# The last twelve chunks of a gated-attention kernel pass the FFN in groups of four, and the second product swaps its operands

## The chip, the cores and the metric

The kernel runs on one NeuronCore of one Trainium2 chip. The metric is the device time of one execution in microseconds; less is better. TensorE (PE) does the matrix products, VectorE (DVE), ScalarE (ACT) and GpSimd (POOL) the elementwise work, and SyncE (SP) issues every DMA of this kernel.

## The reference

Gated linear attention with a state of 48x48 for each head, and then a two-layer feed-forward network (FFN) on all 3072 tokens. Everything is float32.

```python
# q, k, v, alpha: 4 batches, 8 heads, 768 steps, 48 dims
for t in range(S):
    state = alpha[:, :, t, :, None] * state + einsum('bhd,bhe->bhde', k[:, :, t], v[:, :, t])
    y[:, :, t] = einsum('bhd,bhde->bhe', q[:, :, t], state)
x = y.transpose(0, 2, 1, 3).reshape(3072, 384)
h = x @ w_in                       # 384 -> 2048
g = h              where h >= 1
    0              where h <= -1
    (h + 1)**2 / 4 elsewhere
return g @ w_out                   # 2048 -> 384
```

## The kernel before

The 3072 tokens are cut into 24 chunks of 128. `prepare(j)` loads a chunk's alpha, k, q and v and forms running products of alpha with two scans on DVE (L547, L573). `attend(j)` computes the attention of the chunk on PE (transposes L614, scores L629, state updates L642, outputs L769) and `end_chunk` writes it into `ring`, as a high and a low part of each number in the type float32r (L793 on ACT, L798 on DVE). `ring` holds two groups of chunks.

The FFN takes the chunks in groups of `GROUP` = 3, eight groups in all. For each group `n` and each of the 16 slices `f` of 128 hidden units:

- `hidden(n, f)` makes the slice of `h` for the whole group in one PSUM bank, with nine matmuls (L865): three slices of the contraction, and for each the products high x high, low x high and high x low. The stationary operand is a 128x128 piece of `w_in`, the moving one is the group's 384 columns of `ring`. A split, f = 0 of group 0 (`SPLIT` = 1), takes the chunks one at a time, with 128 columns. Then five elementwise operations follow: L909 (DVE), L894 (ACT), L920 (DVE), L924 (ACT, the high part `gh[:, 0]`) and L925 (POOL, the low part `gh[:, 1]`; on DVE for the very last slice).
- `second(seg, f)` adds the slice's part of the output to three PSUM banks `ps_o`, one for each chunk, again with nine matmuls (L943). Here `gh` of one chunk (128x128) is stationary, and the 384 columns of `w_out` move. After the last slice each bank is copied to `ot` (L340, on ACT or DVE) and written to `out` by a DMA (L1002).

Groups 0 and 1 pass the first eight slices before the weights of the other eight are decoded; their partial sums wait in DRAM (`sums`). The weights are fetched and decoded in the first part of the kernel on ACT, DVE and POOL (L365 to L420).

The order of the instructions on each engine is written out by a planner (`Plan.order`). Each operation has a key (for the FFN a running count of slices, for a chunk's attention a due time some `MARGIN` slices before its group begins) and an estimated cost. The planner simulates the engines with these costs and, whenever an engine is free, takes the ready operation with the smallest key. Where PE would rest in the early part, it inserts matmuls on zeros (`fill`, L1014). PSUM's eight banks go to `ps_h` (2), `ps_o` (`GROUP`) and the attention (`6 - GROUP`). If an overflow test fails, a slow version (`stepwise`) is run; it isn't with these inputs.

Of the kernel before, what the change touches and what calls it, by code (L numbers as in the profile page):

```python
# [8 lines left out]
F32 = mybir.dt.float32  # L9
F32R = mybir.dt.float32r  # L10
# [15 lines left out]
SLACK = 2.0**-15  # L26
GROUP = 3
SHARE = 2
# [14 lines left out]
FIRST = 5  # L43
ROOM = 2
# [188 lines left out]
def gated_attention_ffn(ctx: ExitStack, tc: tile.TileContext, q, k, v, alpha, laid, out):  # L233
    nc = tc.nc
    B, H, S, D = q.shape
    P = 128
    DM, DF = H * D, laid["w_out"].shape[0] * laid["w_out"].shape[2] // (H * D) * P
    G = H // 2
    KT = DM // P
    NF = DF // P  # L240
    CH = 128
# [51 lines left out]
    span = lambda n: slice(first[n] % (2 * GROUP), first[n] % (2 * GROUP) + groups[n])  # L293
    meet = const.tile([P, NCH, 2, G], F32, name="meet")
# [5 lines left out]
    segs += [(n, 0, NF) for n in range(NS, NG)]  # L300
    starts = [sum(f1 - f0 for _, f0, f1 in segs[:i]) for i in range(len(segs))]

    begin = {n: starts[[s[0] for s in segs].index(n)] for n in range(NG)}
    need = {}
    for (n, f0, f1), t in zip(segs, starts):
        for f in range(f0, f1):
            need.setdefault(f // NW, t + f - f0)


    wts = ctx.enter_context(tc.tile_pool(name="wts", bufs=2 * NU + MORE))  # L310
    with ExitStack() as main:
# [26 lines left out]

        ps_a = lambda j, *shape: bank("ps_a", 6 - GROUP, [P, *(shape or (G, CH))], FIRST, j < ROOM)
        copy = lambda e, out, in_: (nc.scalar.copy if e == "ACT" else nc.vector.tensor_copy)(out=out, in_=in_)  # L340
# [260 lines left out]
        others, meets, turnt = {}, {}, {}  # L601
        group_of = [max(n for n in range(NG) if first[n] <= j) for j in range(NCH)]

# [182 lines left out]
        def end_chunk(j, ps, key):  # L786

            n = group_of[j]
            xt = ring[:, j % (2 * GROUP)]
            GS = KT if n == 0 else G  # L790
            hi, lo = xt[:, 0:GS, 0], xt[:, 0:GS, 1]
            x_j = ("x", j % (2 * GROUP))
            plan.op("ACT", 0.14 * GS, key, lambda: nc.scalar.copy(out=hi, in_=ps()[:, 0:GS]), [ps], [x_j])  # L793
# [11 lines left out]
            x = ring[:, span(n)].bitcast(F32)  # L805
            all_x = [("x", i % (2 * GROUP)) for i in range(first[n], j + 1)]
            for kt in range(KT):
# [42 lines left out]


        def hidden(n, f, key, c0=0, c1=GROUP):

            c1 = min(c1, groups[n])
            L = (c1 - c0) * CH
            h = bank("ps_h", 2, [P, L])
            gf, gh = buf("fw", "gf", [P, L], 3), buf("fw", "gh", [P, 2, L], 3, F32R)
            xs = [("x", j % (2 * GROUP)) for j in range(first[n] + c0, first[n] + c1)]
# [29 lines left out]

            w = (c1 - c0) / GROUP
            act = lambda in_, func, scale, bias: plan.op(  # L890
# [3 lines left out]
                lambda: nc.scalar.activation(out=gf(), in_=in_(), func=func, scale=scale, bias=bias),  # L894
                [h, gf] if in_ is gf else [h],
                [gf],
            )
            if key < CLIPS:


                act(h, AF.Relu, -0.5, half_b)
                act(gf, AF.Relu, -1.0, ones)
                act(gf, AF.Square, 1.0, 0.0)
            else:
                plan.op(
                    "DVE",
                    0.08 + 0.45 * w,
                    key + 0.4,
                    lambda: nc.vector.tensor_scalar(  # L909
                        out=gf(), in0=h(), scalar1=-1.0, scalar2=1.0, op0=ALU.max, op1=ALU.min  # L910
                    ),
                    [h],
                    [gf],
                )
                act(gf, AF.Square, 0.5, half_b)
# [4 lines left out]
                lambda: nc.vector.tensor_tensor(out=gf(), in0=gf(), in1=h(), op=ALU.max),  # L920
                [gf, h],
                [gf],
            )
            plan.op("ACT", 0.08 + 0.41 * w, key + 0.4, lambda: nc.scalar.copy(out=gh()[:, 0], in_=gf()), [gf], [gh])  # L924
# [4 lines left out]
            plan.op(e, us, key + 0.4, emit, [gf, gh], [gh], port=port, other=None if ends else other)  # L929
            return gh  # L930

        o_ps, seconds, firsts = {}, {}, []

        def second(seg, f, gh, key, c0=0, c1=GROUP):
            n, f0, f1 = seg
            c1 = min(c1, groups[n])
            if f == f0 and c0 == 0:
                o_ps[seg] = [bank("ps_o", GROUP, [P, DM]) for _ in range(groups[n])]

            def product(ts):  # L940
                for t in ts:
                    for i, (a, w) in enumerate(((0, 0), (0, 1), (1, 0))):
                        nc.tensor.matmul(  # L943
                            out=o_ps[seg][t](),
                            lhsT=gh()[:, a, (t - c0) * CH : (t - c0 + 1) * CH],
                            rhs=wout(f, w),
                            start=(f == f0 and i == 0),
                            stop=(f == f1 - 1 and i == 2),
                        )

            ts = range(c0, c1)

            for part in [[t] for t in ts] if f == f1 - 1 else [ts]:
                seconds[seg, f] = plan.op(
                    "PE",
                    0.529 * len(part),
                    key,
                    lambda part=part: product(part),
                    [gh, wo[f // NW]],
                    [o_ps[seg][t] for t in part],  # L960
                    mode="full",
                )
            if f < f1 - 1:
                return
            for t in ts:
                ps, ot = o_ps[seg][t], buf("fw", "ot", [P, DM], GROUP)
                place = ("sums", n, t)
                if f0 > 0:
# [3 lines left out]
                        key - 6,  # L972
                        lambda t=t, ot=ot: nc.sync.dma_start(out=ot(), in_=sums[n, t]),
                        [place],
                        [ot],
                        moved=P * DM * 4,
                        after=[seconds[seg, f - 3]],
                    )
                    plan.op(
                        "DVE",  # L980
                        0.52,
                        key,
                        lambda ps=ps, ot=ot: nc.vector.tensor_tensor(out=ot(), in0=ot(), in1=ps(), op=ALU.add),
                        [ps, ot],
                        [ot],
                    )
                else:
                    plan.op(
                        "ACT",
                        0.45,  # L990
                        key,
                        lambda ps=ps, ot=ot: copy("ACT", ot(), ps()),
                        [ps],
                        [ot],
                        other=("DVE", 0.52, lambda ps=ps, ot=ot: copy("DVE", ot(), ps()), False),
                    )
                r0 = (first[n] + t) * CH
                plan.op(
                    "SP",
                    Plan.ISSUE,  # L1000
                    key,
                    lambda t=t, r0=r0, ot=ot: nc.sync.dma_start(  # L1002
                        out=out[r0 : r0 + CH, :] if f1 == NF else sums[n, t], in_=ot()
                    ),
                    [ot],
                    [place],
                    moved=P * DM * 4,
                )
# [12 lines left out]
        for j in range(NCH):  # L1021
# [6 lines left out]
            while at < len(segs) and first[segs[at][0]] + groups[segs[at][0]] - 1 <= done:  # L1028
                seg, t = segs[at], starts[at]
                at += 1  # L1030
                for f in range(seg[1], seg[2]):
                    key = t + f - seg[1]
                    parts = range(groups[0]) if seg[0] == 0 and f < SPLIT else [0]
# [47 lines left out]
def stepwise(tc, q, k, v, alpha, win, wout, NF, ident, half_b, ones, out):  # L1081
# [8 lines left out]
    with ExitStack() as ctx:  # L1090
# [39 lines left out]
        with tc.For_i(0, B * S, P) as r:  # L1130
# [12 lines left out]
            for kt in range(KT):  # L1143
# [3 lines left out]
                nc.vector.tensor_tensor(out=xt[:, 1, kt], in0=tr, in1=xt[:, 0, kt].bitcast(F32), op=ALU.subtract)  # L1147
            o = ps.tile([P, DM], F32, name="o")
            for f in range(NF):
# [18 lines left out]
                nc.vector.tensor_tensor(out=gh[:, 1], in0=g, in1=gh[:, 0].bitcast(F32), op=ALU.subtract)  # L1168
                for i, (a, w) in enumerate(((0, 0), (0, 1), (1, 0))):
                    nc.tensor.matmul(  # L1170
                        out=o,
                        lhsT=gh[:, a],
                        rhs=wout(f, w),
                        start=(f == 0 and i == 0),
                        stop=(f == NF - 1 and i == 2),
                    )
            ot = sb.tile([P, DM], F32, name="ot2")
            nc.vector.tensor_copy(out=ot, in_=o)
            nc.sync.dma_start(out=out[bass.ds(r, P), :], in_=ot)

# [62 lines left out]
```

## Time and profile before

| | before |
|---|---|
| time, median of 3 runs | 521.03 us (520.73 to 521.82) |
| span of the profiled execution | 520.1 us |
| PE busy | 498.7 us, 96% |
| PE weight loads (PEld) busy | 480.4 us, 92% |
| DVE, ACT, POOL busy | 69%, 51%, 51% |
| granted PE clock | 1.0 of full speed in nearly all of the span |

The page does not give the profiled execution a time of its own beside the span; the median of the three runs is 0.9 us above the span, which is taken for what lies around it. In the views a line such as L943 is line 943 of the kernel before, `x9` counts instructions, and a window A:B is in microseconds from the start of the span. A matmul's own duration runs from its issue to its modelled end and overlaps with the next ones; what one matmul costs in a stream is the distance from start to start.

### The profile page before, as it was taken

Reading aid. Unit: us, or ns where it says so; the run is one execution under the profiler, and the core shown is the slowest. Engines: PE = TensorE matmul, PEld = TensorE weight load, DVE = VectorE, ACT = ScalarE, POOL = GpSimd, SP = SyncE. Lnnn points to the kernel's source line nnn. Section 1 sums busy time; section 2 is a strip of 40 time slices with the busy share of each in tenths; the row PEclk is TensorE's granted clock in tenths of the full one; section 3 lists DMA queues with packets and bytes.
Section 4 is the critical chain, followed back from the end, with each engine's and each line's share of the span. In section 5 each row is a group of like instructions: output and inputs, shape, how many; then the busy total and the mean of one; then the engine's idle time right before and its main releaser. Section 6 shows DMA issues by size and latency. Waiting matters only on the chain.

```text
span 520.1 us, 12248 instructions
## 1 busy us (share of the span) xinstructions
PE 498.7 (96%) x4861; PEld 480.4 (92%) x4861; DVE 359.6 (69%) x673; ACT 262.8 (51%) x509; POOL 262.9 (51%) x286
## 2 busy tenths in 40 slices
PE   8889898979999999999999999999999999999995
PEld 7788788978899999999999999999999999999994
DVE  6999999788978757578567757578567775343333
ACT  3899896575543444344444444444444444333331
POOL 3688885899974354254354344254354242323330
PEclk9999999999999999999999999999999999999999
DMA  8997849011435323133123323133102200010001
GB/s 255 378 348 250 316 98 346 3 48 55 122 106 137 109 65 90 48 96 122 43 60 91 112 62 79 56 84 125 56 21 59 67 2 11 15 37 10 0 1 50
DMA packets 27902, 52.46 MB, mean 101 GB/s; under 512 B 3808, under 2 KB 13504, under 8 KB 27840
## 3 DMA queue, kind: packets, MB, share of 16 engines
q1 hardware_dynamic: 27840, 51.62, 31.8%
q8 instruction: 40, 0.66, 0.6%
q14 instruction: 22, 0.18, 0.1%
HBM read 43.65 MB, written 5.90 MB: 95 GB/s over the span
## 4 chain that ended last, share of the span: by engine, by line
PE 79%; DVE 9%; POOL 4%; issue 3%; ACT 3%; DVEq 0%; POOLq 0%; ACTq 0%
PE ps L943 35%; PE ps L865 34%; PE ps L769 4%; PE ps L642 2%; DVE inv L573 2%; POOL gh L925 2%; PE ps L629 2%; PE ps L614 2%; DVE Q L547 1%; POOL w L405 1%; ACT gf L894 1%; DVE w L381 1%; DVE Q L715 1%; POOL wt L420 1%; PE ps L1014 1%
## 5 line engine op out<-in xcount | busy, mean ns | idle before, releaser
L943 PE MATMUL ps<-wt,gh 128*128 128x384 f32 x1152 | 225.3, 340 | 4.3 <-POOL gh L925 3.5
L925 POOL TENSOR_TENSOR gh<-gf,gh 128x384 fp32r<-128x384 f32 (+1 forms) x129 | 146.6, 1141 | 163.6 <-ACT gh L924 117.2
L865 PE MATMUL ps<-ring,wt 128*128 128x384 f32 (+1 forms) x1170 | 223.0, 337 | 2.8 <-DVE inv L573 1.2
L865 PEld LDWEIGHTS ps<-ring,wt 128*128 128x128 f32 x1170 | 203.9, 188 | 4.3 <-issue 1.5
L943 PEld LDWEIGHTS ps<-wt,gh 128*128 128x128 f32 x1152 | 200.5, 188 | 7.2 <-POOL gh L925 5.2
L894 ACT ACTIVATE gf<-gf,half_b 128x384 f32<-128x384 f32 x122 | 74.6, 616 | 120.7 <-DVE gf L909 117.4
L909 DVE TENSOR_SCALAR gf<-ps 128x384 f32<-128x384 f32 x122 | 66.9, 553 | 71.3 <-PE ps L865 62.7
L920 DVE TENSOR_TENSOR gf<-gf,ps 128x384 f32<-128x384 f32 (+1 forms) x130 | 70.3, 543 | 45.1 <-ACT gf L894 44.7
L924 ACT CAST gh<-gf 128x384 fp32r<-128x384 f32 (+1 forms) x130 | 65.7, 507 | 67.8 <-DVE gf L920 61.1
L573 DVE TENSOR_TENSOR_SCAN inv<-raw,bwd 128x511 f32<-128x511 f32 x17 | 34.9, 2052 | 0.0
L405 POOL TENSOR_TENSOR w<-w,wt 128x384 int32<-128x384 int32 (+1 forms) x25 | 31.2, 1261 | 7.0 <-DVE w L392 6.0
L547 DVE TENSOR_TENSOR_SCAN Q<-raw,fwd 128x512 f32<-128x512 f32 x17 | 27.4, 1613 | 7.3 <-PE ps L769 7.2
L420 POOL TENSOR_TENSOR wt<-w,wt 128x384 fp32r<-128x384 f32 (+1 forms) x24 | 31.3, 1318 | 1.7 <-ACT wt L418 1.4
L661 ACT COPY both<-state 48x192 f32<-48x192 f32 x69 | 24.1, 350 | 12.3 <-POOL state L746 9.0
L746 POOL TENSOR_TENSOR state<-state,last 128x192 f32<-128x192 f32 x20 | 11.9, 594 | 34.3 <-DVE state L671 34.1
L769 PE MATMUL ps<-Q,both 128*64 128x64 f32 x372 | 27.1, 225 | 1.4 <-issue 1.4
L769 PEld LDWEIGHTS ps<-Q,both 128*64 128x64 f32 x372 | 23.7, 137 | 4.1 <-issue 2.8
L769 PE MATMUL ps<-other,both 128*64 128x64 f32 x372 | 27.0, 225 | 0.0
L617 ACT COPY ks<-ps 128x512 f32<-128x512 f32 x24 | 14.1, 587 | 21.5 <-PE ps L614 21.4
L715 DVE TENSOR_TENSOR Q<-ps,mask 64x256 f32<-64x256 f32 x48 | 20.3, 423 | 6.5 <-ACT other L679 5.6
L593 POOL TENSOR_TENSOR Q<-Q,raw 128x512 f32<-128x512 f32 x18 | 23.2, 1290 | 2.9 <-DVE inv L565 2.0
L769 PEld LDWEIGHTS ps<-other,both 128*64 128x64 f32 x372 | 23.5, 138 | 0.2 <-ACT both L661 0.2
(79 smaller groups left out, 415.7 us busy)
## 6 DMA issues: line engine op xcount, KB each, us to landing
both<-in_laid_v_both SPq DMA_DIRECT2D x48, 128.0 KB, 3.0
wt<-in_laid_w_in SPq DMA_DIRECT2D x8, 768.0 KB, 7.2
wt<-in_laid_w_out SPq DMA_DIRECT2D x8, 768.0 KB, 7.5
vt<-in_laid_v SPq DMA_DIRECT2D x24, 192.0 KB, 2.9
out<-ot SPq DMA_DIRECT2D x24, 192.0 KB, 2.7
raw<-in_laid_dim_a SPq DMA_DIRECT2D x17, 256.0 KB, 2.9
raw<-in_laid_dim_k SPq DMA_DIRECT2D x17, 256.0 KB, 3.0
raw<-in_laid_dim_q SPq DMA_DIRECT2D x17, 256.0 KB, 2.7
```

The lines of the kernel that those rows point to most:

```text
L405: add = lambda e, c=c: e.tensor_tensor(out=bits()[:, c], in0=bits()[:, c], in1=word(I32, 0)[:, c], op=ALU.add)
L420: sub = lambda e, c=c: e.tensor_tensor(out=part(1)[:, c], in0=data()[:, c], in1=part(0).bitcast(F32)[:, c], op=ALU.subtract)
L547: lambda: nc.vector.tensor_tensor_scan(flat(Q()), aT(), flat(fwd), 0.0, ALU.mult, ALU.max),
L573: lambda: nc.vector.tensor_tensor_scan(flat(inv())[:, 0:n][:, ::-1], aT()[:, 1 : n + 1][:, ::-1], flat(bwd)[:, 0:n][:, ::-1], bwd[:, G - 1 ...
L769: nc.tensor.matmul(out=ps()[halves[r], to, halves[u]], lhsT=lhsT[:, r, u], rhs=x()[:, g, halves[u]], start=m + u == 0, stop=True, skip_gro ...
L865: nc.tensor.matmul(out=h(), lhsT=win(f, w)[:, kt], rhs=ring[:, at, kt, a, :], start=(m == 0), stop=(m == 3 * KT - 1),)
L894: lambda: nc.scalar.activation(out=gf(), in_=in_(), func=func, scale=scale, bias=bias),
L909: lambda: nc.vector.tensor_scalar(out=gf(), in0=h(), scalar1=-1.0, scalar2=1.0, op0=ALU.max, op1=ALU.min),
L920: lambda: nc.vector.tensor_tensor(out=gf(), in0=gf(), in1=h(), op=ALU.max),
L924: plan.op("ACT", 0.08 + 0.41 * w, key + 0.4, lambda: nc.scalar.copy(out=gh()[:, 0], in_=gf()), [gf], [gh])
L925: sub = lambda e: e.tensor_tensor(out=gh()[:, 1], in0=gf(), in1=gh()[:, 0].bitcast(F32), op=ALU.subtract)
L943: nc.tensor.matmul(out=o_ps[seg][t](), lhsT=gh()[:, a, (t - c0) * CH : (t - c0 + 1) * CH], rhs=wout(f, w), start=(f == f0 and i == 0), sto ...
```

## The change

Groups 0 to 3 stay at three chunks; the last twelve chunks form three groups of four instead of four groups of three. `ring` becomes 2 x 4 chunks long, and its slots go by group. In the second product the operands are swapped: a 128x128 piece of `w_out` is stationary and `gh` of the whole group moves, so that the output comes out transposed (384 x tokens) in three banks `ps_o`, one for each slice of 128 output features; numpy transposes it back on the host. The keys of the planner advance by 4/3 for each slice of a group of four, and the planner's costs are written for both sizes. A smaller scratch area for dynamic DMAs is asked for.

```diff
-GROUP = 3
+SIZES = (3, 3, 3, 3, 4, 4, 4)
+GROUP = max(SIZES)
...
-    groups = [min(GROUP, NCH - j) for j in range(0, NCH, GROUP)]
+    groups = list(SIZES)
...
+    slot = lambda j: group_of[j] % 2 * GROUP + j - first[group_of[j]]
+    span = lambda n: slice(slot(first[n]), slot(first[n]) + groups[n])
...
+    unit = [c / 3 for c in groups]
+    starts = [sum((f1 - f0) * unit[n] for n, f0, f1 in segs[:i]) for i in range(len(segs))]
...
-        sums = pools["sums"].tile([max(NS, 1), GROUP, P, DM], F32, name="sums")
+        sums = pools["sums"].tile([max(NS, 1), KT, P, GROUP * CH], F32, name="sums")
...
-        ps_a = lambda j, *shape: bank("ps_a", 6 - GROUP, ...
+        ps_a = lambda j, *shape: bank("ps_a", 6 - KT, ...
...
+        cost = lambda c: 9 * max(c * 0.0533 + 0.0155, 0.111)
...   (in hidden)
-                    (0.529 if c1 - c0 > 1 else 0.7) * (c1 - c0),
+                    cost(c1 - c0),
...   (in second)
-                o_ps[seg] = [bank("ps_o", GROUP, [P, DM]) for _ in range(groups[n])]
+                o_ps[seg] = [bank("ps_o", KT, [P, groups[n] * CH]) for _ in range(KT)]
-            def product(ts):
-                for t in ts:
+            def product(ms):
+                for m in ms:
                     for i, (a, w) in enumerate(((0, 0), (0, 1), (1, 0))):
                         nc.tensor.matmul(
-                            out=o_ps[seg][t](),
-                            lhsT=gh()[:, a, (t - c0) * CH : (t - c0 + 1) * CH],
-                            rhs=wout(f, w),
-                            start=(f == f0 and i == 0),
+                            out=o_ps[seg][m]()[:, c0 * CH : c1 * CH],
+                            lhsT=wout(f, w)[:, m * P : (m + 1) * P],
+                            rhs=gh()[:, a, 0 : (c1 - c0) * CH],
+                            start=(f == f0 and i == 0 and c0 == 0),
                             stop=(f == f1 - 1 and i == 2),
...
-                    0.529 * len(part),
+                    cost(c1 - c0) / KT * len(part),
...
-                        out=out[r0 : r0 + CH, :] if f1 == NF else sums[n, t], in_=ot()
+                        out=out[m * P : (m + 1) * P, cols] if f1 == NF else sums[n, m, :, 0:L], in_=ot()
...   (on the host)
-    nc = bacc.Bacc("TRN2", target_bir_lowering=False, num_devices=1)
+    nc = bacc.Bacc("TRN2", target_bir_lowering=False, num_devices=1, dynamic_dma_scratch_size=1024)
-    return r.results[0]["out"]
+    return np.ascontiguousarray(r.results[0]["out"].T)
```

## Rows read from the trace of the kernel before

**Rows 1.** The page's parts 1 and 4: busy time by engine, and the chain of work that ended last, by engine and by line.

```profile
PE 498.7 (96%) x4861; PEld 480.4 (92%) x4861; DVE 359.6 (69%) x673; ACT 262.8 (51%) x509; POOL 262.9 (51%) x286
PE 79%; DVE 9%; POOL 4%; issue 3%; ACT 3%; DVEq 0%; POOLq 0%; ACTq 0%
```

**Rows 2.** Busy time of each engine in stretches of the span, with the granted clock, the share of the DMA engines and GB/s.

```profile
30.00:36.00 6.00, 4.66 (x114) 3.86 (x109) 5.79 (x12) 5.85 (x15) 4.55 (x6) 1.00 1.04 358
42.00:48.00 6.00, 5.36 (x108) 4.74 (x104) 5.54 (x8) 5.88 (x12) 5.19 (x7) 1.00 0.62 188
48.00:54.00 6.00, 4.38 (x38) 4.06 (x40) 5.56 (x14) 5.86 (x12) 4.99 (x6) 1.00 0.93 360
...
80.00:120.00 40.00, 35.00 (x279) 33.22 (x278) 33.88 (x57) 26.62 (x48) 33.65 (x27) 1.00 0.36 128
120.00:130.00 10.00, 9.29 (x52) 8.61 (x51) 9.08 (x10) 5.60 (x9) 10.00 (x6) 1.00 0.01 2
...
235.40:294.30 58.90, 58.90 (x591) 57.63 (x590) 40.36 (x80) 26.69 (x55) 24.98 (x28) 1.00 0.28 80
360.00:420.00 60.00, 60.00 (x597) 58.73 (x596) 41.43 (x84) 27.22 (x56) 25.02 (x29) 1.00 0.18 53
420.00:480.00 60.00, 60.00 (x437) 59.11 (x436) 27.05 (x51) 24.30 (x44) 19.51 (x20) 1.00 0.06 16
```

**Rows 3.** The chain of work that ended last in the stretch 440:470, pieces in order of time: start, duration, what.

```profile
441.25 1.57 PE ps L865 x9
442.82 1.57 PE ps L943 x9
...
467.99 1.57 PE ps L943 x9
469.57 0.53 PE ps L865 x3
```

**Rows 4.** From the timelines of PE: fills of 256 columns in bf16 (start, duration from the first start to the last end, count).

```profile
11.96 2.25 PE L1014 MATMUL ps<-zeros 128*128 128x256 bf16 x19
```

**Rows 5.** The chain in the early part, 22 to 30 us and 39 to 45 us: products of 128 columns, and what the chain runs through where the first slices pass.

```profile
24.51 0.95 PE ps L865 x9
26.54 1.15 PE ps L865 x9
...
40.42 0.59 ACT gf L894
41.03 0.63 ACT gf L894
41.68 0.53 ACT gf L894
42.20 0.83 ACT w L365
43.03 0.47 ACT gf L894
43.50 0.73 ACT wt L418
```

**Rows 6.** Groups of DVE and POOL instructions in 235.4:294.3, one period of three chunks: busy us, mean ns | idle before.

```profile
L909 DVE TENSOR_SCALAR gf<-ps 128x384 f32<-128x384 f32 x16 | 8.8, 553 | 8.9 <-PE ps L865 6.4 <-POOL gh L925 2.0 <-POOL both L664 0.5
L920 DVE TENSOR_TENSOR gf<-gf,ps 128x384 f32<-128x384 f32 x16 | 8.7, 546 | 5.2 <-ACT gf L894 5.1
L798 DVE TENSOR_TENSOR ring<-ps,ring 128x512 fp32r<-128x512 f32 x3 | 2.0, 672 | 0.0
L340 DVE COPY ot<-ps 128x384 f32<-128x384 f32 x2 | 1.1, 558 | 0.3 <-PE ps L943 0.3
L925 POOL TENSOR_TENSOR gh<-gf,gh 128x384 fp32r<-128x384 f32 x16 | 18.1, 1135 | 22.1 <-ACT gh L924 13.8 <-issue 8.3
```

**Rows 7.** The chain in 500:521, and from the timeline of that stretch the last slice's elementwise chain and the issue of the last output DMAs.

```profile
507.33 1.57 PE ps L865 x9
508.90 0.35 PE ps L943 x2
509.25 0.26 PE ps L1053 x2
509.50 4.57 PE ps L943 x25
514.10 0.56 DVE ot L340
...
509.01 0.56 DVE L909 TENSOR_SCALAR gf<-ps 128x384 f32<-128x384 f32 x1 [1.35 <-PE ps L865]
511.44 0.56 DVE L925 TENSOR_TENSOR gh<-gf,gh 128x384 fp32r<-128x384 f32 x1 [0.63 <-ACT gh L924]
513.64 2.27 SPq L1002 DMA_DIRECT2D out<-ot  x3
```

**Rows 8.** DMA issues by line: count, KB each, median us from issue to landing.

```profile
out<-ot SPq DMA_DIRECT2D x24, 192.0 KB, 2.7
ring<-ring SPq DMA_DIRECT2D x42, 48.0 KB, 2.2
```

More of the change, by code (lines that the diff above doesn't have):

```diff
@@ L287, in gated_attention_ffn @@
     PER = S // CH
-    groups = [min(GROUP, NCH - j) for j in range(0, NCH, GROUP)]
+    groups = list(SIZES)
+    assert sum(groups) == NCH
     NG = len(groups)
@@ L292, in gated_attention_ffn @@
     ring = const.tile([P, 2 * GROUP, G, 2, CH], F32R, name="ring")
-    span = lambda n: slice(first[n] % (2 * GROUP), first[n] % (2 * GROUP) + groups[n])
+    group_of = [max(n for n in range(NG) if first[n] <= j) for j in range(NCH)]
+    slot = lambda j: group_of[j] % 2 * GROUP + j - first[group_of[j]]
+    span = lambda n: slice(slot(first[n]), slot(first[n]) + groups[n])
     meet = const.tile([P, NCH, 2, G], F32, name="meet")
@@ L805, in end_chunk @@
             x = ring[:, span(n)].bitcast(F32)
-            all_x = [("x", i % (2 * GROUP)) for i in range(first[n], j + 1)]
+            all_x = [("x", slot(i)) for i in range(first[n], j + 1)]
             for kt in range(KT):
@@ L912, in hidden @@
                     [h],
-                    [gf],
+                    [gf_t],
                 )
@@ L928, in hidden @@
             (e, us, emit, port), other = reversed(ways) if ends else ways
-            plan.op(e, us, key + 0.4, emit, [gf, gh], [gh], port=port, other=None if ends else other)
-            return gh
+            plan.op(e, us, key + 0.4, emit, [gf_t, gh_t], [gh_t], port=port, other=None if ends else other)
+            return gh_t
         o_ps, seconds, firsts = {}, {}, []
@@ L959, in second @@
                     [gh, wo[f // NW]],
-                    [o_ps[seg][t] for t in part],
+                    [o_ps[seg][m] for m in part],
                     mode="full",
@@ L964, in second @@
                 return
-            for t in ts:
-                ps, ot = o_ps[seg][t], buf("fw", "ot", [P, DM], GROUP)
-                place = ("sums", n, t)
+            L, w = groups[n] * CH, groups[n] / 3
+            cols = slice(first[n] * CH, first[n] * CH + L)
+            for m in ms:
+                ps, ot_t = o_ps[seg][m], buf("fw", "ot", [P, GROUP * CH], KT)
+                ot = lambda ot_t=ot_t: ot_t()[:, 0:L]
+                place = ("sums", n, m)
                 if f0 > 0:
@@ L993, in second @@
                         [ps],
-                        [ot],
-                        other=("DVE", 0.52, lambda ps=ps, ot=ot: copy("DVE", ot(), ps()), False),
+                        [ot_t],
+                        other=("DVE", 0.1 + 0.42 * w, lambda ps=ps, ot=ot: copy("DVE", ot(), ps()), False),
                     )
-                r0 = (first[n] + t) * CH
                 plan.op(
@@ L1168, in stepwise @@
                 nc.vector.tensor_tensor(out=gh[:, 1], in0=g, in1=gh[:, 0].bitcast(F32), op=ALU.subtract)
[L1169 to L1179, printed above, removed]
+                for m in range(KT):
+                    for i, (a, w) in enumerate(((0, 0), (0, 1), (1, 0))):
+                        nc.tensor.matmul(
+                            out=o[m],
+                            lhsT=wout(f, w)[:, m * P : (m + 1) * P],
+                            rhs=gh[:, a],
+                            start=(f == 0 and i == 0),
+                            stop=(f == NF - 1 and i == 2),
+                        )
+            for m in range(KT):
+                ot = sb.tile([P, P], F32, name=f"ot2{m}")
+                nc.vector.tensor_copy(out=ot, in_=o[m])
+                nc.sync.dma_start(out=out[m * P : (m + 1) * P, bass.ds(r, P)], in_=ot)
 _INS = ["q", "k", "v", "alpha"]
@@ L1237 @@
     b, h, s, d = inputs["q"].shape
-    o = nc.dram_tensor("out", (b * s, h * d), F32, kind="ExternalOutput").ap()
+    o = nc.dram_tensor("out", (h * d, b * s), F32, kind="ExternalOutput").ap()
     with tile.TileContext(nc, schedule_with_timeline_sim=True) as tc:
```

56 lines of the change are left out of this document (28 added, 28 removed).

## The prediction

> **What bounds the kernel now.** The page first: PE is busy 96% of the span, PE's pieces make up 79% of the chain that ended last, and DVE has 9% of it [rows 1]. A busy PE need not be the bound, so the windows come next: they show two regimes. Up to about 140 us PE rests: 5.0 of the 40 us from 80 to 120, while DVE has 33.9 and POOL 33.7 of them, and from 120 to 130 POOL is busy without a break [rows 2]. There the decoding of the weights and the first attention compete, and PE waits for them. From there to the end of the products PE is busy in every microsecond of each window, at the full clock, with DVE at 0.69 (41.43 of 60 us), and at 0.45 once the attention is over [rows 2]. In this second regime only PE work counts: what a PE instruction is shortened by comes off the end, and what DVE, ACT, POOL and the DMAs gain or lose is free as long as PE doesn't run dry. The last twelve chunks lie wholly in it.
>
> The chain in the quiet stretch then gives the price of the work that the change touches. From 441.25 to 469.57 it holds nothing but 18 groups of nine matmuls, L865 and L943 in turn: 28.32 / 162 = 174.8 ns for each matmul of 384 columns [rows 3]. L865 and L943 cost the same, though one streams `ring` and the other `w_out`, so swapping which operand is stationary is taken as free by itself. At the granted clock of 1.00, the level of 2.4 GHz, 384 columns are 160.0 ns. So 14.8 ns of each matmul are something else.
>
> **The change, part by part.**
>
> *Products of the last twelve chunks.* Before, four groups x 16 slices x 18 matmuls = 1152, at 174.8 ns: 201.4 us. After, three groups x 16 x 18 = 864, each of 512 columns, which nothing in the trace shows. The columns alone are 213.3 ns. The three ways to add the rest: if the 14.8 ns are paid once for each matmul, 228.1 ns and 197.1 us, a gain of 4.3 us (288 matmuls x 14.8 ns). If they go with the columns, 174.8 x 4/3 = 233.1 ns, the same 201.4 us and no gain. If the longer stream covers what sticks out now, as in the fills (2.25 us for 19 matmuls of 256 columns; less 0.28 us for the last one's own run this is 109 ns from start to start, only 2.8 ns over the 106.7 ns of their columns [rows 4]), 216.1 ns and 186.7 us, a gain of 14.7 us. I take the first. What is the same for every matmul, of 384 or 512 columns, is one weight load of 128x128; and the fills show that columns by themselves stream at the clock's rate with nearly nothing added. The row that the value comes from, L865 and L943 at 384 columns, is also the nearest in kind (float32r), while the fills are bf16. Gain 4.3 us, bounds 0 and 14.7.
>
> The fills' small surplus has a counterpart in the Trainium skill (TensorE: Matmul & The Clock Gate, Back-to-back issue gap): a warm matmul takes its columns at 2.4 GHz plus about 2.5 ns. By that page 384 columns would take 162.5 ns, and the trace has 174.8, so the page misses 12.3 ns here; with its figure alone as the part paid once, the sum would be a gain of 288 x 2.5 ns, an estimate of 0.7 us.
>
> *The split slice at the start.* The second product of slice 0 in group 0 goes chunk by chunk. Before: 9 matmuls of 384 columns, 1.57 us. After: for each chunk three banks, 27 matmuls of 128 columns. The same kind, L865 with 128 columns, takes 0.95 and 1.15 us for nine, so 27 take 2.9 to 3.5 us: 1.3 to 1.9 us more PE work near 39 to 44 us [rows 5]. What hides it: PE rests there (1.3 us in 30:36, 0.6 in 42:48, 1.6 in 48:54 [rows 2]), and the chain in that place runs through ACT's L894, L365 and L418, not through PE [rows 5]. The products that queue behind it feed those same ACT operations, which are late already. I take 0.3 us; with the cover gone it is 1.9.
>
> *The planner's order.* Its costs change a little (three chunks, 1.579 for 1.587; the split pieces, more). Keys and due times up to the first group of four are the same. So the order up to 140 us can differ in places, where waits of PE between 0.6 and some 2 us stand now. No row prices this; I put it at nothing, with 1.5 us to either side as an allowance.
>
> *Attention of the last twelve chunks.* It is the same work, but while group 3 passes (still three chunks) four chunks are to be prepared instead of three. One period of three chunks takes 58.9 us, of which 32 groups of nine, 50.3 us, are FFN, so a chunk's attention is 2.9 us of PE. DVE is busy 40.4 us of it; 8.8 + 8.7 + 1.1 us are L909, L920 and L340, so a chunk takes 7.3 us [rows 2, 6]. With four: 18.6 + 4 x 7.3 = 47.7 us of DVE in 61.8 us, 77%. POOL: 18.1 + 4 x 2.3 = 27.3 us, 44%. Nothing there is nearly full, so PE should not run dry. While groups 4 and 5 pass, four chunks again stand beside four, as three beside three now.
>
> *Elementwise work at 512 columns.* A DVE read of PSUM with 384 columns takes 553 ns, with 512 it takes 672 (L798) [rows 6], so each of the five operations grows by some 0.12 us, POOL's L925 (1135 ns) by 0.4 at most in proportion: about 0.9 us more from the end of `hidden` to a complete `gh`. Three `second` operations are outstanding after the last `hidden` (2 + 25 = 27 matmuls of L943 [rows 7]), so four groups of nine pass between a slice's `hidden` and its `second`: 6.3 us now, 8.2 then. The slack grows faster than the latency: nothing.
>
> *The tail.* The last `hidden` ends at 508.90, and its `gh` is complete at 512.0 (511.44 + 0.56), 3.1 us later. The two `second` operations before it cover 3.15 us. With 512 columns the chain grows by five times 0.12 us (L925 is on DVE there) to 3.7 us, and the cover to 4.1: nothing. After the last matmul come the last copy, 0.56 us now [rows 7], 0.68 then, and its DMA, of 256 KB instead of 192: by the rows for 48 and 192 KB (2.2 and 2.7 us to landing [rows 8]) 0.2 us more. Together 0.3 us.
>
> *At nothing:* `ring` moves (L814) become 36 DMAs for 42, output DMAs 21 for 24, all on SP, in stretches where the DMA engines are at 0.18 and 0.06 [rows 2]; PSUM keeps 2 + 3 + 3 banks; one boundary between groups fewer, at which PE shows no wait; the smaller DMA scratch (every DMA in the rows is issued by SP); the host's transposition is outside the metric. If a boundary cost one copy of a bank to a following product, that would be 0.68 us each, three times.
>
> **Sum.** 520.1 - 4.3 + 0.3 + 0.3 = 516.4 us of span. The median of the runs lies 0.9 us above the span, so 517.3 us, a ratio of 0.993.
>
> **Rivals.**
>
> *The surplus goes with the columns.* A float32r stream could run a little below one column per cycle; L865 and L943 agree in 14.8 ns and have the same length, so they cannot tell. Against it speak the fills, in another type. Between all of it (gain 0) and all but the fills' 2.8 ns (gain 0.8): 520.8 to 521.6 us, no change. The same result as by the page's figure above. Chance 0.14.
>
> *The longer stream swallows the surplus.* 521.0 - 14.7 + 0.6 = 506.9 us. For it: the fills; against it: 160 ns of columns do not swallow it now, in either line. Chance 0.04.
>
> *The early part comes out worse.* The split slice in full (1.9 us) and the allowance for the order (1.5) instead of 0.3: 520.4 us. Chance 0.07, within 0.2% or a little faster.
>
> *Attention becomes late: the other side.* The place is the passing of group 3. If DVE, with four chunks, came to be as full as from 80 to 120 us (33.9 of 40, 85%) with POOL as full, PE would rest as it does there, 5.0 of 40 us: 7.7 us in 61.8, so 525.0 us. It makes the kernel slower from 4.8 us of rest on, and begins to matter when chunk 15's `ring` is written after group 4's first slice is due. Against it: 77% and 44%. Chance 0.05.
>
> **How the numbers follow.** The forecast has 0.70, its own range 515.8 to 518.8 (the allowance of 1.5 us for the early part). The range for 8 in 10 takes in the worse early part and the near edge of the first rival: 515.8 to 520.8. A difference under 0.2%, 1.0 us, can hardly be told from none by a measurement of this kernel. Faster: the forecast, the swallowed surplus (0.04), half of the worse early part, 0.02 of the first rival: 0.79. Same: 0.16. Slower: 0.05.
>
> **What the profile after would show.** L943 and L865 at 512 columns in the last stretch: nine in 2.05 us if right, 2.10 if the surplus goes with columns, 1.94 if it vanishes. PE without a rest from about 140 us to the last product, also where group 3 passes; a wait of L865 for `ring` or its DMAs (L814) there would speak for late attention. DVE and ACT: fewer, longer operations, without effect. The prediction is wrong if the dense regime starts more than 2 us later than before, or if the price of 512 columns is not 228 ns.

## The result and the profile after

The change made the kernel a little slower: 525.0 us (median; 523.0 to 525.5) against 521.3, a ratio of 1.0065 with an interval of 1.0049 to 1.0081. Measured again beside the experiments on another chip it was 523.2 against 521.4, 1.0051 (1.0034 to 1.0068). A ratio is taken over all executions and is not quite that of the two medians. The forecast was 517.3 us, with 515.8 to 520.8 as its range. The profiled execution has a span of 522.9 us where before had 520.1.

The page's parts 1 and 4 of the changed kernel; L872 and L950 are now the first and the second product:

```profile
PE 500.9 (96%) x4601; PEld 442.5 (85%) x4601; DVE 352.8 (67%) x638; ACT 255.9 (49%) x475; POOL 257.9 (49%) x272
PE 72%; POOL 9%; ACT 7%; DVE 5%; issue 4%; DMA 2%; POOLq 0%; DVEq 0%
```

PE has 260 matmuls fewer than in [rows 1] and is busy 2.2 us longer, where the forecast had the products of the last twelve chunks take 4.3 us less. So the wider matmuls must be dearer than forecast. The chain in the last stretch, pieces in order of time, shows by how much (it answers to [rows 3]):

```profile
440.51 2.10 PE ps L872 x9
442.61 2.10 PE ps L950 x9
...
465.71 2.10 PE ps L872 x9
467.81 2.10 PE ps L950 x9
```

From 440.51 to 467.81 there are 13 groups of nine: 27.30 / 117 = 233.3 ns for 512 columns, not 228.1. That is 864 x 233.3 = 201.6 us, against 201.4 before: the gain is gone. The second loss is in the windows (columns as in [rows 2]) and in the waits of PE from 195 to 300 us (us in total, times, longest):

```profile
200.00:260.00 60.00, 58.64 (x649) 56.26 (x649) 42.59 (x87) 26.85 (x57) 26.89 (x29) 1.00 0.34 97
...
420.00:480.00 60.00, 60.00 (x285) 48.36 (x284) 21.43 (x32) 20.03 (x30) 17.40 (x14) 1.00 0.08 20
...
PE ps L618 <- DVE inv L592: 1.4, 3, 0.5
```

Beside group 3, where four chunks are prepared, PE rests 1.4 us, in three waits of the key transposition L618 for DVE's `inv`. DVE is busy 71% there: it is not full. The third loss lies before: the first product of group 2 (the 307th matmul of L872, of L865 before) starts at 167.1 us, and at 165.8 before.

The end of the chain, to set beside [rows 7], and the span from issue to landing of the three last output DMAs (least, median, most):

```profile
510.53 5.95 PE ps L950 x25
516.48 0.02 issue
516.50 0.69 DVE ot L345
...
DMA to landing us min/median/max: 2.1/2.1/4.0
```

PE's last product ends 2.4 us later than before (516.48 for 514.08). The sum: 1.3 for the start, 1.4 beside group 3, 0.2 for the products, and about 0.4 back, since L950 takes 1.56 us for nine of 384 columns in groups 2 and 3 where L943 took 1.573. The last DMA here landed 4.0 us after its issue; in the second profile of the same program it was 2.4, and that accounts for 1.6 of the 2.1 us between these two executions (525.0 and 522.9 us). The time of one program differs by some 2 us between executions (e14 below: five of 517.8 to 518.1 and two of 520.3 to 520.4 us), so the ends of PE's work are compared below. Around the span lie 2.1 us with the change and, on the chips of the experiments, 1.7 with the kernel before.

### The profile page after: what moved, and what is told of

It reads as the page before. It is cut to its first block, busy times and chain, and to the rows that moved or that the text cites. A ratio compares the mean times of both kernels' runs of the same rounds, so it can differ in the third digit from the quotient of the medians.

```text
span 522.9 us, 11571 instructions
## 1 busy us (share of the span) xinstructions
PE 500.9 (96%) x4601; PEld 442.5 (85%) x4601; DVE 352.8 (67%) x638; ACT 255.9 (49%) x475; POOL 257.9 (49%) x272
## 4 chain that ended last, share of the span: by engine, by line
PE 72%; POOL 9%; ACT 7%; DVE 5%; issue 4%; DMA 2%; POOLq 0%; DVEq 0%
PE ps L950 32%; PE ps L872 31%; PE ps L773 4%; POOL wt L425 3%; POOL gh L932 3%; POOL w L410 2%; PE ps L646 2%; PE ps L633 1%; ACT wt L378 1%; PE ps L618 1%; DMA wt<-in_laid_w_in 1%; ACT gf L901 1%; ACT w L370 1%; DMA both<-in_laid_v_both 1%; DVE inv L578 1%
## 5 line engine op out<-in xcount | busy, mean ns | idle before, releaser
L950 PE MATMUL ps<-gh,wt 128*128 128x384 f32 (+2 forms) x1026 | 223.6, 363 | 5.0 <-POOL gh L932 3.0
L932 POOL TENSOR_TENSOR gh<-gf,gh 128x384 fp32r<-128x384 f32 (+2 forms) x113 | 141.9, 1258 | 169.5 <-ACT gh L931 132.3
L872 PE MATMUL ps<-ring,wt 128*128 128x384 f32 (+2 forms) x1026 | 222.0, 362 | 1.3 <-ACT wt L378 0.9
L950 PEld LDWEIGHTS ps<-gh,wt 128*128 128x128 f32 x1026 | 181.5, 188 | 26.9 <-POOL gh L932 4.3
L872 PEld LDWEIGHTS ps<-ring,wt 128*128 128x128 f32 x1026 | 182.9, 188 | 21.2 <-ACT wt L378 1.2
L901 ACT ACTIVATE gf<-gf,half_b 128x384 f32<-128x384 f32 (+1 forms) x106 | 70.5, 666 | 103.6 <-DVE gf L916 99.6
L916 DVE TENSOR_SCALAR gf<-ps 128x384 f32<-128x384 f32 (+1 forms) x106 | 64.9, 613 | 75.3 <-PE ps L872 69.0
L931 ACT CAST gh<-gf 128x384 fp32r<-128x384 f32 (+2 forms) x114 | 62.8, 552 | 79.8 <-DVE gf L927 68.0
L927 DVE TENSOR_TENSOR gf<-gf,ps 128x384 f32<-128x384 f32 (+2 forms) x114 | 67.8, 597 | 45.5 <-ACT gf L901 45.2
L425 POOL TENSOR_TENSOR wt<-w,wt 128x384 fp32r<-128x384 f32 (+1 forms) x24 | 30.6, 1286 | 3.2 <-ACT wt L423 2.8
L552 DVE TENSOR_TENSOR_SCAN Q<-raw,fwd 128x512 f32<-128x512 f32 x17 | 23.1, 1361 | 5.9 <-PE ps L773 5.8
```

The source lines that it names most:

```text
L425: sub = lambda e, c=c: e.tensor_tensor(out=part(1)[:, c], in0=data()[:, c], in1=part(0).bitcast(F32)[:, c], op=ALU.subtract)
L872: nc.tensor.matmul(out=h(), lhsT=win(f, w)[:, kt], rhs=ring[:, at, kt, a, :], start=(m == 0), stop=(m == 3 * KT - 1),)
L916: lambda: nc.vector.tensor_scalar(out=gf(), in0=h(), scalar1=-1.0, scalar2=1.0, op0=ALU.max, op1=ALU.min),
L950: nc.tensor.matmul(out=o_ps[seg][m]()[:, c0 * CH : c1 * CH], lhsT=wout(f, w)[:, m * P : (m + 1) * P], rhs=gh()[:, a, 0 : (c1 - c0) * CH], ...
```

## The experiments

**The disputed price by itself (e1).** A kernel with no attention and no FFN, only streams of 45 matmuls at several widths, each matmul with its own weight load:

```diff
+        for i in range(N):
+            nc.tensor.matmul(out=banks[1], lhsT=st[:, i % 4], rhs=mv, start=(i == 0), stop=(i == N - 1))
...   (the same with 448, 384, 256 and 128 columns, with strided and zero operands, and in bf16)
```

> Streams of 45 matmuls alone on TensorE, each with its own 128x128 weight load, no attention and no FFN; the output is zeros. Theory (the part of a float32r matmul over its columns' time goes with the columns): from start to start 233 ns at 512 columns, 204 at 448, 175 at 384, 117 at 256, and about 106 at 128 where the weight load sets the pace; bf16 near the columns' time, 216, 163, 109. Rival 1 (a fixed 14.8 ns, and something of the full kernel makes 512 columns slower there): 228 at 512 alone on TensorE, 201 at 448, 121 at 256. Rival 2 (a full PSUM bank, or the strided reading of the ring, costs extra): 448 columns on the line through 384, 512 above it, or the strided stream slower than the contiguous one.

The chain of e1, one piece for each stream: float32r with 512, 448, 384, 256, 128 columns, 512 strided as `ring` is, 512 zeros; then bf16 with 384, 256, 128.

```profile
19.10 10.23 PE b L45 x45
29.33 9.12 PE b L47 x45
38.45 7.82 PE b L49 x45
46.27 5.39 PE b L51 x45
51.66 4.98 PE b L53 x45
56.64 10.28 PE b L55 x45
66.92 10.20 PE b L57 x45
77.11 7.33 PE b L59 x45
84.44 4.91 PE b L61 x45
89.36 2.51 PE b L63 x45
```

The three streams of 512 columns give 10.20 to 10.28 / 45 = 226.7 to 228.4 ns; the larger figures hold the change from the stream before, and from start to start the last 30 of each have 226.7. The narrower ones give 202.7, 173.8, 119.8 and 110.7. Less the columns at 2.4 GHz that is 13.4 ns at 512, 16 at 448, 13.8 at 384 and 13.1 at 256; only at 128 is it far more, 57. So a float32r matmul alone does pay about 13.3 ns once at 256, 384 and 512 columns (why 448 has 2.7 more was not looked into), as the forecast had it, and my theory of the moment, that it goes with the columns, fell. At 128 columns PEld, which loads the weights, is busy in the whole stream; that it sets the pace there is likely, but no run tests it. In bf16 it is 162.9, 109.1 and 55.8 ns, 2.4 to 2.9 over the columns. The formula of the Trainium skill (TensorE: Matmul & The Clock Gate, Back-to-back issue gap) gives a warm matmul by itself a gap of its columns plus 2.5 ns: bf16 agrees, here in a stream; float32r, with about 13.3, does not. Neither zeros nor strides change the price. Something in the full kernel takes 6.6 ns more for each matmul of 512 columns.

**Where the operands lie (e5, e11).** e5 changes one thing of the stream for each run of 54, e11 moves the start of both operands in SBUF, in bytes after a multiple of 512.

```diff
-            nc.tensor.matmul(out=banks[1], lhsT=st[:, i % 4], rhs=mv[:, 0], ...
+            nc.tensor.matmul(out=banks[5], lhsT=st[:, i % 4], rhs=all_mv[:, 8:520], ...     # e5: 32 bytes further
...
+    piece = lambda i, s: st[:, s // 4 + 128 * (i % 8) : s // 4 + 128 * (i % 8) + 128]       # e11
+    move = lambda m, n: mv[:, m // 4 : m // 4 + n]
```

> Streams of 54 float32r matmuls of 512 columns alone on TensorE, the output is zeros; each stream changes one thing towards the kernel: 54 different stationary pieces, one piece only, moving operand shifted by 64, 32 and 960 bytes, larger values, a moving operand that alternates, groups of nine over changing PSUM banks, all of it together, and all of it at 384 columns. The first streams alone settled at 227 ns, the changed kernel takes 233. Theory A (where the two operands lie in memory decides): 233 in one of the shifted streams or with 54 pieces, 227 in the others. Theory B (changing banks or operands every few matmuls costs it): 233 in the streams with groups of nine or alternating operand. Theory C (what else goes on in the kernel does): 227 in all.

> Streams of 40 float32r matmuls alone on TensorE, output zeros: the start of the moving operand lies 0 to 448 bytes, that of the stationary pieces 0 to 224 bytes, after a multiple of 512. Theory (only the distance between the two counts): 227 ns at 512 columns wherever both are shifted alike, more where they differ; with (moving, stationary) as in the changed kernel, (224, 0) and (64, 0), 233; at 384 columns (0, 64) and (224, 0), as before, 174.8, and (0, 0) 173.3. Rival (the moving operand's own place counts): (64, 64) and (224, 224) as slow as (64, 0) and (224, 0), and (0, 64) as fast as (0, 0).

e5's chain: 54 different stationary pieces, moving operand 64, 32 and 960 bytes further, groups of nine over changing banks.

```profile
39.42 12.24 PE b L47 x54
...
63.90 12.38 PE b L51 x54
76.28 12.59 PE b L53 x54
88.87 12.60 PE b L55 x54
...
125.96 12.24 PE b L61 x54
```

12.24 / 54 = 226.7 ns; the other streams of 512 columns have 226.7 to 227.2, but for the shifted ones, with 229.3, 233.1 and 233.3. Theory A stands, B and C fall. e11 maps it. Its chain, with (moving, stationary) at (0, 0), (32, 0), (64, 0), (128, 0), (192, 0), (224, 0), (256, 0), (320, 0), (384, 0), (448, 0), (64, 64), (224, 224), (0, 64), and then 384 columns at (0, 0), (64, 0), (0, 64), (224, 0):

```profile
20.66 9.08 PE b L45 x40
29.75 9.34 PE b L47 x40
39.08 9.16 PE b L49 x40
48.24 9.29 PE b L51 x40
57.53 9.33 PE b L53 x40
66.86 9.33 PE b L55 x40
76.19 9.09 PE b L57 x40
85.28 9.17 PE b L59 x40
94.46 9.29 PE b L61 x40
103.75 9.34 PE b L63 x40
113.08 9.12 PE b L65 x40
122.21 9.11 PE b L67 x40
131.32 9.34 PE b L69 x40
...
159.05 6.96 PE b L75 x40
166.01 6.93 PE b L77 x40
172.94 7.06 PE b L79 x40
180.00 6.94 PE b L81 x40
```

227 to 228 ns at (0, 0), (256, 0), (64, 64) and (224, 224); 229 at (64, 0) and (320, 0); 232 to 233.5 at (32, 0), (128, 0), (192, 0), (224, 0), (384, 0), (448, 0) and (0, 64). So in these streams the price follows the moving start less the stationary one, modulo 256 bytes: 64 and 320 agree, 128 and 384, and 192, 448 and (0, 64). At 384 columns it is 173.3 to 174.0 at (0, 0), (64, 0) and (224, 0), and 176.5 at (0, 64). In the compiled programs, before and after alike, the weights begin at a multiple of 512 bytes, `ring` 224 and `gh` 64 bytes after one (the traces hold no addresses; this was read from the programs). For L872, at (224, 0), the map gives 233, as measured. For the other lines it misses: L950, at (64, 0), should have 229 and takes 233, and before, at 384 columns, L865 at (224, 0) should have 173.5 and L943 at (0, 64) 176.5, where both take 174.8. The map shows that the places count; what each line of the full kernel pays it doesn't give, and why stays open.

The Trainium skill (TensorE: Matmul & The Clock Gate, Step-by-step: what each phase is for) says that PE has two independent read ports and that loading the next weights takes no bandwidth from the running matmul. In the streams a matmul with a weight load of its own takes up to 6.7 ns longer by the places of its two operands alone. That the two readings get in each other's way there is a guess; no run here shows through what the places act.

**The operands moved, in the full kernels (e9, e14, e10b, e13).** The same program with `ring` and `gh` at multiples of 512 bytes; e9 and e14 are the changed kernel, e10b the one before (with the smaller scratch area, to make room), e13 the changed one with eight groups of three. In each, `flag` and `meet` come ahead of `ring`, and 448 bytes of padding go ahead of `gh`.

```diff
+    flag = const.tile([1, 1], I32, name="flag")
+    meet = const.tile([P, NCH, 2, G], F32, name="meet")
     ring = const.tile([P, 2 * GROUP, G, 2, CH], F32R, name="ring")
...
+        pools["fw"].tile([P, 112], F32, name="pad", bufs=1)
...   (e13 too)
-SIZES = (3, 3, 3, 3, 4, 4, 4)
+SIZES = (3, 3, 3, 3, 3, 3, 3, 3)
```

> The changed kernel with ring and gh moved in SBUF so that they begin at a multiple of 512 bytes, as the weights do; the order and all operations stay. Theory (the distance of the two operands in memory made 512 columns cost 233 ns): nine products of 512 columns in 2.04 us instead of 2.10, 864 x 6.6 ns = 5.7 us, and the time 5 to 6 us below the changed kernel, 3 to 4 below the kernel before. Rival (something else of the kernel): 2.10 us for nine, no change.

> The kernel before with ring and gh at multiples of 512 bytes (and the smaller scratch area, to make room, which alone changed nothing). Theory (the distance of the operands costs 1.5 ns for each matmul of 384 columns too): nine in 1.560 us, 2304 x 1.5 ns = 3.4 us less than before, about 518 us. Rival (at 384 columns the place hardly counts in the kernel): equal to before.

> Eight groups of three with the operands swapped as in the change, and ring and gh at multiples of 512 bytes: beside the placed kernel with groups of four this is the effect of 512 columns alone. Theory (13.3 ns of each matmul are paid once, whatever its columns, when the places are right): the last twelve chunks take 1152 x 173.3 = 199.6 us against 864 x 226.7 = 195.9, and there is no wait of 1.4 us beside group 3, so TensorE ends 2.3 us later than with placed groups of four. Rival (what was gained by the places is the same for both widths): the two differ by the wait alone, with groups of three 1.4 us faster.

> The changed kernel with ring and gh placed, once more, beside the other three on one chip. All theories: about 519.9 us, as measured before.

| | nine products | group 2 begins | last product ends | from one to the other | time | ratio to before |
|---|---|---|---|---|---|---|
| before | 1.57 us | 165.8 | 514.1 | 348.3 | 521.3 | |
| changed, first profile | 2.10 | 167.1 | 516.5 | 349.4 | 525.0 | 1.0065 (1.0049 to 1.0081) |
| changed, second profile | 2.10 | 166.6 | 516.0 | 349.4 | 523.2 | 1.0051 (1.0034 to 1.0068) |
| changed, placed (e9) | 2.04 | 168.4 | 513.0 | 344.6 | 519.9 | 0.9967 (0.9949 to 0.9985) |
| changed, placed (e14) | 2.04 | 166.5 | 511.1 | 344.6 | 518.0 | 0.9935 (0.9911 to 0.9959) |
| before, placed (e10b) | 1.56 | 165.8 | 511.9 | 346.2 | 518.9 | 0.9942 (0.9920 to 0.9963) |
| swapped, groups of three, placed (e13) | 1.56 | 166.7 | 513.7 | 347.0 | 522.7 | 1.0001 (0.9979 to 1.0023) |

Two pieces of the chain of e14, in the stretch of [rows 3], and the last products of e14 and e13:

```profile
441.23 2.04 PE ps L874 x9
443.27 2.04 PE ps L952 x9
...
505.18 5.91 PE ps L952 x25
```

```profile
509.09 4.58 PE ps L952 x25
513.67 0.02 issue
```

Moving the operands takes the nine from 2.10 to 2.04 us, 226.7 ns a matmul, and 4.8 us off the stretch from group 2 to the last product. From the first product of group 4, where the 512 columns begin, to the end of the last it takes 227.5 us in all five profiles of programs with groups of four and unmoved operands (also e3, e6 and e7 below) and 222.8 in all three with moved ones (also e12). This is the cause of the lost gain, shown; 864 x 6.6 ns, the expected, would be 5.7; where the other 1 us is stays open.

e9 and e14 are one program. e9's time fell short of what was expected of it, since it began group 2 late, 1.9 us after e14. In its trace the granted clock drops in the early part; the first row is e9's, the second that of the changed kernel's second profile:

```profile
0.00:40.00 40.00, 35.44 (x578) 30.18 (x578) 33.05 (x68) 28.56 (x61) 24.09 (x43) 0.96 0.98 317
0.00:40.00 40.00, 36.11 (x592) 30.69 (x592) 34.15 (x70) 28.97 (x63) 24.13 (x43) 1.00 0.96 320
```

The drop lies in 35 to 40 us: a mean of 0.66 of full speed, so part of it at the lower level of 1.2 GHz, and PE worked on 54 matmuls in those 5 us, where e14 has 68 at 1.00. In the 5 us before, PE was busy 3.80 us in both.

e13 against e14 then shows the forecast term itself: with right places, groups of four take 2.4 us less than groups of three from group 2 to the end, for an expected 2.3 (288 x 13.3 ns = 3.8, less the 1.5 us of waits that e14 still has). The kernel before had paid for its places too, 2.1 us by the end of PE's work and 2.8 by the medians. The 3.4 expected counted all 2304 matmuls; the 1728 of groups 2 to 7, which pass where PE doesn't rest, are 2.6. e13 isn't faster than before, though its nine take 1.56: it begins group 2 0.9 us later, and takes 0.8 us more from there than e10b, of which 0.2 is a wait; the rest stays open.

**The swap of operands, and the scratch area (e2, e4, e8).** e2 is the changed kernel with `SIZES` all three, e4 the one before with `dynamic_dma_scratch_size=1024`, e8 is e2 with the second product of slice 0 made once for three chunks.

> The changed kernel with eight groups of three: operands of the second product swapped as in the change, no groups of four. Theory (512 columns give nothing; the loss is about 1.1 us from the start, about 1.4 us of waits while four chunks are prepared beside a group of three, and some 1 us outside the span): no wait of TensorE from 150 us on, span about 521.2 us, time about 1 to 2 us below the changed kernel. Rival (the swap of operands itself costs in the dense part): span 522 to 523 us, as changed.

> The kernel before with only the smaller scratch area for dynamic DMAs. Theory (the scratch area changes what lies around the span: 2.1 us after the change against some 0.9 before): about 1.2 us slower than before at the same span. Rival (the scratch area does nothing, as no DMA of this kernel uses it): equal to before within 0.3 us.

> Eight groups of three with the operands of the second product swapped, and the second product of slice 0 made once for the three chunks. Theory (the swap saves about 0.9 ns for each matmul of the second product, 1152 of them, and the start is repaired): about 1 us faster than before. Rival (the start stays as late as with the changed kernel's groups of three): equal to before.

e2: 521.7 us against 521.6 (1.0012, 0.9991 to 1.0032), PE's last product at 514.0, and 0.2 us of waits from 140 us on in place of the 1.4. So neither the swap nor the split slice makes the dense part slower; the groups of four do. The swap even makes it faster: from the first product of group 2 (at 166.6 us) to the end of the last, e2 takes 347.4 us, before 348.3, and the later start takes the 0.9 us back. e4: 521.4 us, ratio 1.0008 (0.9992 to 1.0025): the scratch area does nothing. e8: 522.3, 1.0016 (1.0005 to 1.0028); the repaired split slice made nothing faster: group 2 began at 168.6 us, 2.9 later than before, which is the rival and more.

**The start (e3, e6).** e3 gives the planner its old costs of PE products; e6 is the changed kernel with the second product of slice 0 made once, nine matmuls of 384 columns for 27 of 128.

```diff
-                    cost(c1 - c0),
+                    (0.529 if c1 - c0 > 1 else 0.7) * (c1 - c0),
...   (in second)
-                    cost(c1 - c0) / KT * len(part),
+                    0.529 * (c1 - c0) / KT * len(part),
```

> The changed kernel with the planner's costs of PE products as before (0.529 for each chunk, 0.7 for a chunk of the split slice), so that only the order differs. Theory (the start is late because the order there changed with the costs): first product of group 1 and of group 2 about 1 us earlier than in the changed kernel, time about 1 us less. Rival (it is late because the split slice now takes 27 short matmuls): no difference beyond 0.5 us.

> The changed kernel in which slice 0 of group 0 still makes its hidden units chunk by chunk, but passes the second product once for all three chunks: 9 matmuls of 384 columns instead of 27 of 128. Theory (the late start comes from these short matmuls): group 1 to 3 begin about 0.8 us earlier and the time falls by as much. Rival (the order of the early part differs for other reasons): less than 0.3 us.

> The changed kernel once more, beside the others on one chip, so that the experiments are compared with it. All theories: slower than before by 2 to 4 us.

The first product of group 2 starts at 165.8 us before, 167.1 and 166.6 in the two profiles of the change, 166.0 in e3 and 167.6 in e6. By the profiles of all runs, the programs with the planner's old costs begin it at 165.8 to 166.0 us (before, e3, e4, e10b, e12), those with the new costs and the 27 short matmuls at 166.5 to 167.1 (the two of the change, e2, e13, e14), or later where the clock dropped (e7 and e9). e3's PE ends 0.5 us before the second profile of the change, but its time, 523.3 (1.0029, 1.0015 to 1.0043), does not show the 1 us expected. e6 is the slowest of the experiments, 525.2 (1.0073, 1.0056 to 1.0090). In it the second eight slices of group 0 began 3.5 us earlier, at 102.1 us, and the lead was lost again by 166 us, in PE's waits (whole span):

```profile
PE ps L618 <- DVE inv L592: 5.5, 8, 1.2
PE ps L952 <- POOL wt L425: 4.7, 3, 1.8
```

The waits for decoded weights (POOL, L425), 0.7 us in the changed kernel, are 4.7 here: what PE gains early, it waits for later. The short matmuls are not the cause (e3 has them and begins at 166.0); the order that follows from the planner's costs is worth some 0.6 to 1.1 us.

**The waits beside group 3 (e7).** The planner's costs of the two scans, for the last twelve chunks only, nearer to what they take.

```diff
-                1.2,
+                1.2 if j < 12 else 1.4,
...
-                1.25,
+                1.25 if j < 12 else 1.9,
```

> The changed kernel with the planner's costs of the two scans of the last twelve chunks nearer to what they take (1.4 and 1.9 us for 1.2 and 1.25). Theory (the waits of 1.4 us while four chunks are prepared beside a group of three come from an order made with scans that are too short): TensorE's rest between 195 and 300 us falls below 0.3 us, time about 1 us less than the changed kernel. Rival (DVE is simply too full there): the waits stay above 1 us.

The windows of e7:

```profile
195.00:260.00 65.00, 65.00 (x777) 62.95 (x776) 45.80 (x94) 31.04 (x64) 28.46 (x34) 1.00 0.31 92
```

PE has no rest at all there, with DVE busy 0.70 of it as before. The rest had come from an order written with scans that were too short, not from a full DVE. From the first product of group 2 to the end of the last, e7 takes 347.4 us, the changed kernel 349.4. The time, 522.9 us (1.0016, 0.9994 to 1.0038), is only 0.4 below the changed kernel's, less than the 1 expected: in its profile group 2 began at 167.9 us, 1.2 later, after a granted clock of 0.69 in 35 to 40 us, as in e9, and the last DMA's landing alone differs by 1.6 between executions.

**All three together (e12).** The changed kernel with the places of e9, the costs of e3 and those of e7.

> The changed kernel with ring and gh placed, with the planner's costs of PE products as before, and with scan costs nearer to what they take for the last twelve chunks. Theory (the three losses are separate: places 4.7 us as measured, waits beside group 3 1.4 us, order of the start about 1 us): 2 to 2.5 us less than the placed kernel, about 517.5 us, faster than both kernels. Rival (they overlap; a start that is earlier is lost again where PE waits for DVE and POOL): within 1 us of the placed kernel.

515.05 us against 521.7: 0.9876 (0.9852 to 0.9900), the fastest of all, 6.6 us below the kernel before. PE's work ends at 508.6 us, 2.5 before e14, as the theory of separate losses had it: 0.6 from a start at 165.9 us, and 2.0 from there on, where it takes 342.6 us. Beside e10b (346.2), in which PE has no waits there either, the groups of four are 3.6 us ahead, for the 3.8 of 288 x 13.3 ns.

```profile
200.00:260.00 60.00, 60.00 (x683) 58.27 (x682) 44.90 (x89) 27.74 (x58) 27.49 (x30) 1.00 0.31 92
...
502.63 5.91 PE ps L952 x25
508.55 0.02 issue
```

## Why the prediction was wrong

*The bound* was right: from 140 us on PE's own work sets the end, and what took PE's time (233.3 ns) or its rest (1.4 us) showed at the end in full.

*The price of 512 columns* is the step that failed: 228.1 ns, a gain of 4.3 us, where the kernel has 233.3 and a loss of 0.2. That is 4.5 of the 7.7 us between 517.3 and 525.0; 1.4 are the waits beside group 3, 1.0 the start beyond its 0.3, 1.2 what lies around the span, and the swap gave 0.4 back. The measured price is that of the first rival, 233.1, so "the surplus goes with the columns" gave the right number for the wrong reason. Alone on PE the surplus is paid once, and 512 columns cost 226.7 ns. The step took 14.8 ns as a property of the kind of matmul; it was 13.3 ns of that and 1.5 of where the operands lie (e10b), and the second part grew to 6.6 at 512 columns (e9, e14). No row of before could show it: both of its products were of one width, and each in one place. The lower bound of the gain, 0, was all but the value; the chance of 0.14 was too small for it, as no row bore on the question.

*Swapping the operands* was taken as free; it gained about 0.4 us in groups 2 and 3 of the changed kernel and 0.9 us in the six groups of e2 that pass in the dense part, which e2's time doesn't show, as its start was later by as much.

*The attention beside group 3* was put at nothing because DVE would be 77% full. It was 71% full and PE still rested 1.4 us. The last rival named the place and asked for a full DVE; that it gave 525.0 us, the very time measured, is luck, since its 7.7 us of rest were 1.4. A fixed order needs less: three transpositions stood a little too early, since the planner's scans were too short (e7).

*The start* was put at 0.3 us, with up to 1.5 more for the order. It came to 0.8 to 1.3 us, and e3 and e6 put it to the order, for which the sum had nothing and the allowance 1.5; the split slice that the step had priced costs no more than its 0.3 (e3 and e12 begin group 2 at most 0.2 us after before).

*The tail* was put at 0.3 us and its PE part was right: the last `gh` came in time (L950 ran its 25 in 5.95 us without a rest). The landing of the last DMA moves by 1.6 us between executions, which the step did not know. *Around the span* 0.9 us were taken for both kernels, from the median of three executions and the span of one; where both are known for one execution, they are 1.7 for the kernel before and 2.1 for the changed one. The scratch area is not the cause of the difference (e4), and e3, e6 and e7, which have groups of four, have 1.7 to 1.8 again. What is, stays open.

## What to carry to other kernels

A price per instruction that is read from one shape in one place holds for that shape and place: before resting a gain of 15 ns an instruction on it, measure the new shape by itself and then look at what the full kernel adds. Where float32r matmuls with a weight load each are what bounds a kernel, try it with the stationary and the moving tile at the same offset modulo 256 bytes; here moving `ring` and `gh` was worth 2.8 us to the kernel before, and without it the regrouping lost 2 to 4 (bf16 was not tried). In a kernel whose order comes from estimated costs, every changed cost is a change of its own: three waits of half a microsecond stood where DVE was 71% busy.

## What the hardware showed that was not expected

- A float32r matmul of 512 columns with a weight load of its own takes 226.7 to 233.5 ns at the full clock, by the distance modulo 256 bytes between the starts of its two operands in SBUF; at 384 columns 173.3 to 176.5 ns (e5, e11).
- float32r pays about 13.3 ns over its columns for each matmul at 256, 384 and 512 columns, bf16 2.4 to 2.9 at 128, 256 and 384 (e1); at 128 columns float32r takes 110.7 ns and bf16 55.8.
- Output DMAs of 256 KB at the end of the kernel landed 2.1 to 4.0 us after their issue in one execution and 2.1 to 2.4 in another of the same program.
- One program began its dense part up to 1.9 us later in an execution whose granted clock fell to 0.66 in 35 to 40 us (e9 beside e14); a drop to 0.68 in 115 to 120 us cost e12 nothing that its start at 165.9 us shows (PE rests 4.7 of the 40 us from 80 to 120 there).
